# A decode step with a long KV cache: VectorE's loop border moved by half a block, two reorderings on VectorE and TensorE, and wider output rows

## The chip, the cores and the metric

The kernel runs on one core of a Trainium2 chip. The metric is device time in microseconds (us), the median of several executions of the whole program. A profile of one further execution shows when each instruction ran and when each transfer landed.

## The reference

One token (batch 1, sequence 1, width 1024) goes through an attention over a cache and a small mixer with an MLP, side by side, both from the same normalised input:

```python
def _A_ref(x, k_cache, v_cache, wq, wo):          # 32 query heads, 4 KV heads, 65536 keys, width 128
    q = (x @ wq).reshape(B, Sq, Hq, Dh) ...
    scores = jnp.einsum("bhqd,bhkd->bhqk", q, k) * (Dh ** -0.5)
    p = _softmax(scores, axis=-1)
    o = jnp.einsum("bhqk,bhkd->bhqd", p, v)
    return o... .reshape(B, Sq, Hq * Dh) @ wo

def _B_ref(x, w1, w2, w3, w4):
    h = _gelu(_layernorm(x, axis=-1) @ w1)
    ...                                            # shifts along the sequence, here of one token
    x1 = x + hs
    h2 = _gelu(_layernorm(x1, axis=-1) @ w3) @ w4  # 1024 -> 3584 -> 1024
    return x1 + h2

x = A_x
xn = _layernorm(x, axis=-1)
return x + _A_ref(xn, A_k_cache, A_v_cache, A_wq, A_wo) + _B_ref(xn, B_w1, B_w2, B_w3, B_w4)
```

Everything is bf16. The two caches are 67 MB each, and eight query heads share a KV head, so every byte of K and V is read once and used for eight short products.

## The kernel before

**Tiles and blocks.** The keys of a KV head are cut into 8 tiles of 8192, which makes `NT` = 32 tiles `n` for the 4 heads. Four tiles make a block. A block's V is one load of 8 MB into one of two V slots (`issue_v`, L335). Its K is two loads of 4 MB, one for tiles 0 and 1 of the block into K slot 0 and one for tiles 2 and 3 into K slot 1 (`issue_k`, L325). All loads go through SyncE's queue in program order, and each waits there until its slot is free: a K slot when the scores of its second tile have been computed, a V slot when the last products with it have.

**One tile**, in the order in which the loop (L580) writes it down:

- `Ttr(n, ...)` (L484) lets VectorE transpose the tile's K in place, in four pieces of 128x1024 (L489). K must be turned before TensorE can use it.
- `QK(n)` (L492) is 16 products on TensorE that write the scores to `S_ps`.
- `stats1`, `MB` and `stats2` find a bound for the exponents: VectorE takes the row maximum (L506) and spreads it (`Rm`, L507), TensorE combines the rows in a small product (L512), VectorE takes the minimum (L516).
- `EXP(n)` (L519) updates the running bound `brun` on VectorE, and ScalarE takes the exponentials into `p_sb` (L527).
- `PTr(n)` (L533) permutes them on TensorE (L535) and transposes them on VectorE (L537) into `pT_f`.
- `PV(n)` (L539) is 16 products with V on TensorE into `OT_ps`.
- `FLASH(n)` (L550) copies the result on ScalarE and adds it, rescaled, to `O_acc` on GpSimd. After 8 tiles `head_end` (L561) puts the head's result away, on GpSimd too.

**The order of the work** is written out by hand: each engine executes its own instructions strictly in the order of this loop, and waits on semaphores where it needs another engine or a load. VectorE works ahead: while tile `n` goes through its chain, the pieces of tile `ahead` = `n + 1` are transposed in between, the first one ahead of `stats1(n)`, the second behind `EXP(n)`, the last two behind `PTr(n)`. This is done within a block alone; the first tile of a block is transposed in one go at the block's start:

```python
if n % 4 == 0:
    q_dve.mark(const_sems)
    q_act.mark()
    Ttr(n, range(4))
ahead = n + 1 if n % 4 < 3 else None
```

**The loops.** `mark` (L49) notes where a loop's body begins. `emit_looped` (L68) turns the stretches between marks into a hardware loop, whose iterations must have the same instructions; what lies ahead of the first mark and behind the last is emitted straight. VectorE and ScalarE loop over blocks of four tiles, TensorE and GpSimd over heads of eight.

**The end.** Behind the last tile come the products with w1, w2 and w3 (`quad_rows`), the normalisation of the attention, and the output rows. `out_rows` (L448) multiplies one column (128 values of `gh_bf`, the MLP's hidden vector, or of `o_bf`, the attention's result) with a row of 1024 weights, as four products of 256 columns side by side in the four column groups of TensorE, each accumulating into its own partition of `OUT_ps`. `w4` has 28 such rows, in three loads of 16, 10 and 2 rows; `wo` has 32 in one load. The order on TensorE is 16 rows of `w4`, the 32 of `wo`, 10 and then 2 rows of `w4` (L671 to L674). The loads land in the same order. Then VectorE copies the sum (L675) and one transfer writes the output.

Of the kernel before, what the change touches and what calls it, by code (L numbers as in the profile page):

```python
# [7 lines left out]
F32 = mybir.dt.float32  # L8
ACTF = mybir.ActivationFunctionType
ALU = mybir.AluOpType  # L10
# [127 lines left out]
def _op(q, fn, reads=(), writes=(), partial=False, tick=True):  # L138
    _deps(q, reads, writes)
    ev = q.op(fn, tick)  # L140
    _done(ev, reads, writes, partial)
    return ev


def _grp(q, fns, reads=(), writes=(), partial=False):
    _deps(q, reads, writes)
    ev = None
    for i, fn in enumerate(fns):
        ev = q.op(fn, i == len(fns) - 1)
    _done(ev, reads, writes, partial)  # L150
    return ev
# [16 lines left out]
def bass_parallel_sum__gqa_block_cached__mixer_s_mlp__decode_kernel(  # L168
# [13 lines left out]
    P = 128  # L182
    D = A_x.shape[2]
# [9 lines left out]
    NT = HKV * NSUB  # L193
# [7 lines left out]
    with ExitStack() as es:  # L201
        E = es.enter_context

        def sb(name, shape, dt):
            return E(nc.sbuf_tensor(name, shape, dt))
# [8 lines left out]
        ones_f = sb("ones_f", [P, P], F32)  # L214
# [15 lines left out]
        xn3 = sb("xn3", [P, KT_D], F32)  # L230
        xn3_bf = sb("xn3_bf", [P, KT_D], BF)
        ln_s = sb("ln_s", [P, 8], F32)
        spare = sb("spare", [P, 4], F32)
        ln_xc = sb("ln_xc", [P, KT_D], F32)
        ln_sq = sb("ln_sq", [P, KT_D], F32)
        qT_bf = sb("qT_bf", [P, HQ], BF)
# [13 lines left out]
        ff = sb("ff", [P, 2], F32)  # L250
        cb_rL = sb("cb_rL", [P, HKV], F32)
        cb_o = sb("cb_o", [P, 32], F32)
        o_bf = sb("o_bf", [P, 32], BF)
        acc = sb("acc", [P, KT_D], F32)
        g_bf = sb("g_bf", [P, KT_D], BF)
        gh_bf = sb("gh_bf", [P, KT_F], BF)
        KV = sb("KV", [P, 98304], BF)
# [12 lines left out]
        OUT_ps = ps("OUT_ps", [P, 512], F32)  # L270
        S_ps = ps("S_ps", [P, 512], F32)
# [8 lines left out]
        q_pe = _Q("pe", sem("c_pe"), in_order=True)  # L280
        q_dve = _Q("dve", sem("c_dve"))
        q_act = _Q("act", sem("c_act"))
        q_pool = _Q("pool", sem("c_pool"))
# [11 lines left out]
        b_const = _B("const")  # L295
# [4 lines left out]
        b_V = [_B(), _B()]  # L300
        b_tmpO = _B(); b_tmpL = [_B(), _B()]; b_epi = _B(); b_CM = _B()
        b_S = _B(); b_PT = _B(); b_MB = _B(); b_OT = _B()
# [6 lines left out]
        b_OUT = _B()  # L309
        b_cb = _B()  # L310
        b_o = _B()
# [89 lines left out]
        for c0, n_, lhs, rhs in ((0, P, selGT[:, :], selGT[:, :]), (P, P, selGT[:, :], selPT[:, :]),  # L401
                                 (256, 4, selTT[:, :], ident_bf[0:4, 0:4]), (260, 16, selDT[:, :], ident_bf[0:16, 0:16])):
            _op(q_pe, lambda e, c0=c0, n_=n_, lhs=lhs, rhs=rhs: e.matmul(CM_ps[:, c0:c0 + n_], lhs, rhs, start=True, stop=True),
                reads=[b_const, b_pT], writes=[b_CM], partial=(c0 > 0))
# [7 lines left out]
        for j in range(KT_D):  # L412
            for b in range(2):
                for jj in range(4):
# [3 lines left out]
                        start=(j == 0), stop=(j == KT_D - 1), tile_position=(0, 32 * jj)))  # L418
# [9 lines left out]
        for h in range(HKV):  # L428
            for we in range(4):
# [3 lines left out]
                    reads=[b_M1, b_const], writes=[b_Y], partial=(h + we > 0))  # L433
# [3 lines left out]
        def head_switch(h):  # L437

            _deps(q_pool, [b_Y], [b_Yc])
            src = (lambda: Yall[:, HKV - 1, :, :, :]) if h == 0 else (lambda: Yall[:, bass.ds(q_pool.var, 1), :, :, :].rearrange("p o a b g -> p (o a) b g"))  # L440
            ev = q_pool.op(lambda e: e.tensor_copy(Ycur[:, :, :, :], src()), tick=(s_y, h + 1))
            _done(ev, [b_Y], [b_Yc])
            for b in (b_brun[1],):
                for s, v in list(b.w.items()) + list(b.r.items()):
                    q_pool.wait((s, v))
            q_pool.ops.append((2, lambda e: e.memset(brun[:, 1:2], BIG), s_b, 2))

        def out_rows(items, reads, last=False):  # L448
            fns = []
            for lhs, rhs in items:  # L450
                for jj in range(4):
                    fns.append(lambda e, lhs=lhs, rhs=rhs, jj=jj: e.matmul(  # L452
                        OUT_ps[32 * jj:32 * jj + 1, 0:256], lhs, rhs[:, 256 * jj:256 * jj + 256],
                        start=False, stop=last, tile_position=(0, 32 * jj), skip_group_check=True))
            _grp(q_pe, fns, reads=reads, writes=[b_OUT], partial=True)
# [26 lines left out]
        pT_bf = pT_f[:].bitcast(BF).rearrange("p (q r two) -> p q r two", q=16, two=2)  # L482

        def Ttr(n, idx):  # L484
            s, half = (n // 2) % 2, n % 2
            for ix in idx:
                c = KOFF[s] // 2 + 4096 * half + 1024 * ix
                _deps(q_dve, [b_K[s][half]], [])
                ev = q_dve.op(lambda e, c=c: e.transpose(out=KV32[:, c:c + 1024], in_=KV32[:, c:c + 1024]))  # L489
                b_T[s][half].add_write(ev)  # L490

        def QK(n):  # L492
            s, half = (n // 2) % 2, n % 2
            fns = []
            for we in range(4):
                w_hi, e_ = divmod(we, 2)
                for cm in range(4):
                    mv = bass.AP(KV[:].tensor, KOFF[s] + half * 8192 + cm * 128 + w_hi * 64 + e_, [[kstep, P], [512, 16], [2, 32]])
                    fns.append(lambda e, we=we, cm=cm, mv=mv: e.matmul(  # L499
                        S_ps[32 * cm:32 * cm + 32, :], Ycur[:, we, :, :].rearrange("p a g -> p (a g)"), mv,  # L500
                        start=(we == 0), stop=(we == 3), tile_position=(0, 32 * cm)))
            _grp(q_pe, fns, reads=[b_T[s][half], b_Yc], writes=[b_S])
# [36 lines left out]
        def PV(n):  # L539
            s, r = (n // VSUB) % 2, n % VSUB  # L540
            v0 = VOFF[s] + 8192 * r
            fns = []
            for q in range(16):
                q4 = q % 4
                fns.append(lambda e, q=q, q4=q4: e.matmul(OT_ps[32 * q4:32 * q4 + 32, :], pT_bf[:, q, :, 1],  # L545
                                                          KV[:, v0 + 512 * q:v0 + 512 * (q + 1)],
                                                          start=(q < 4), stop=(q >= 12), tile_position=(0, 32 * q4)))
            _grp(q_pe, fns, reads=[b_pT, b_V[s]], writes=[b_OT])

        def FLASH(n):  # L550

            m = n % 2
            _op(q_act, lambda e: e.activation(tmpO[:, 1:513], OT_ps[:, :], ACTF.Copy), reads=[b_OT], writes=[b_tmpO])  # L553
            _deps(q_pool, [b_ff[m]], [b_Oacc])
            q_pool.op(lambda e: e.tensor_tensor(out=spare[:, 0:1], in0=ff[:, m:m + 1], in1=ff[:, m:m + 1], op=ALU.add), False)  # L555
            b_Oacc.set_write(q_pool.op(lambda e: e.tensor_scalar(out=O_acc[:, :], in0=O_acc[:, :], scalar1=ff[:, m:m + 1], scalar2=0.0, op0=ALU.mult, op1=ALU.add)))  # L556
            _deps(q_pool, [b_tmpO, b_tmpL[m], b_Oacc], [])
            ev = q_pool.op(lambda e: e.tensor_tensor(out=O_acc[:, m:m + 513], in0=O_acc[:, m:m + 513], in1=tmpO[:, m:m + 513], op=ALU.add), tick=(s_fl, n + 5))  # L558
            _done(ev, [b_ff[m], b_tmpO, b_tmpL[m]], [b_Oacc])
# [20 lines left out]
        for n in range(NT):  # L580
            if n % NSUB == 0:
                q_pe.mark(const_sems)
                q_pool.mark()
            if n % 4 == 0:
                q_dve.mark(const_sems)
                q_act.mark()
                Ttr(n, range(4))
            ahead = n + 1 if n % 4 < 3 else None
            QK(n)
            if ahead:  # L590
                Ttr(ahead, [0])
            stats1(n)
            MB(n)
            stats2(n)
            EXP(n)
            if ahead:
                Ttr(ahead, [1])
            PTr(n)
            if ahead:
                Ttr(ahead, [2, 3])  # L600
            if n % NSUB == NSUB - 1:
                head_switch(n // NSUB + 1)
            PV(n)
            FLASH(n)
            if n % NSUB == NSUB - 1:
                head_end(n // NSUB)
            if n % 2:
                issue_k((n + 3) // 2)
            if n % 4 == 1:
                issue_v((n + 3) // 4)  # L610
            if n == NT - 3:
                load_at(KOFF[0], b_K[0][:1] + b_T[0], "w1", B_w1, 0, 8)
                load_at(KOFF[0] + 8192, b_K[0][1:], "w2", B_w2, 0, 8)
                b_epi.r.update(b_V[0].r)
                load_at(VOFF[0], [b_V[0]], "w3", B_w3, 0, 8)
            if n == NT - 1:
                load_at(KOFF[1], b_K[1] + b_T[1], "w40", B_w4, 0, 16)
                load_at(VOFF[1], [b_V[1]], "wo", A_wo, 0, 32)
        for q in (q_pe, q_pool, q_dve, q_act):
            q.mark(const_sems)  # L620

        quad_rows(M0_ps, [b_M0], (xn2_bf, b_xn2), KV[:, 0:8192], b_K[0][0], 256)
# [24 lines left out]
                        b_w.add_read((s, v))  # L647
                load_at(c0, [b_w], "w4%d" % i, B_w4, r0, nr)

        def w4_pe(i):  # L650
            r0, nr, c0, b_w = w4_parts[i]
            out_rows([(gh_bf[:, r:r + 1], KV[:, c0 + (r - r0) * D:c0 + (r - r0 + 1) * D]) for r in range(r0, r0 + nr)], [b_w, b_gh], last=(i == len(w4_parts) - 1))

        _op(q_dve, lambda e: e.tensor_copy(EPI[:, 1024:1280], CM_ps[:, 0:256]), reads=[b_CM], writes=b_ge)
        _op(q_pe, lambda e: e.matmul(MB_ps[:, 0:HKV], Dmat_f, keep[:, :, P], start=True, stop=True), reads=[b_keep] + b_ge, writes=[b_MB])
# [12 lines left out]
        _op(q_dve, lambda e: e.transpose(out=ghT, in_=MM_ps[:, :].rearrange("p (b c) -> p b c", b=2)[:, :, 0:448].rearrange("p b (i r) -> p r b i", r=28)),  # L668
            reads=[b_M0, b_M1], writes=b_ge)
        gelu(tmp_flat[:, 0:896:32], KT_F, gh_bf[:, :], b_ge, [b_gh], (ge_x, ge_a, ge_b), b_ge)  # L670
        w4_pe(0)  # L671
        out_rows([(o_bf[:, r:r + 1], wo_sb[:, r * D:(r + 1) * D]) for r in range(32)], [b_V[1], b_o])
        w4_pe(1)
        w4_pe(2)  # L674
        _op(q_dve, lambda e: e.tensor_copy(orow, OUT_ps[:, 0:256]), reads=[b_OUT], writes=[b_p[0]])  # L675
        ev_out = _dma(q_sp, chan("out"), lambda e: e.dma_start(out=out[0, 0, :].rearrange("(j n) -> j n", j=4), in_=orow[0:97:32, :]), reads=[b_p[0]])
        q_sp.wait(ev_out)
# [34 lines left out]
```

## Time and profile before

| | |
|---|---|
| time, median of 3 runs (range) | 409.73 us (408.55 to 411.58) |
| profiled execution: its own time | 412.34 us |
| profiled execution: span from first to last instruction | 410.8 us |
| busy: VectorE, TensorE, GpSimd, ScalarE | 230.7, 167.0, 91.8, 49.6 us |
| read from memory | 169.87 MB, 414 GB/s over the span |
| mean granted TensorE clock | 0.605 of full speed |
| one transpose of a K piece (L489), 128 of them | 1.21 us |
| K load, from issue to landing (median of 16) | 21.7 us |
| V load, from issue to landing (median of 8) | 33.5 us |

A row of the groups names line, engine and operation, then output and input with their shapes, and gives the mean duration of one. Idle time is followed by what ended it. Times in the timelines are us from the span's start. Loads and engines run beside each other, so the busy times don't add up to the span.

### The profile page before, as it was taken

The numbers are of one execution on the slowest core, as the hardware profiler recorded it, in microseconds if no ns is written. First come the engines' busy times: TensorE is split into PE (matmuls) and PEld (weight loads), VectorE is DVE, ScalarE is ACT, GpSimd is POOL, SyncE is SP. The second block draws the span as 40 slices with busy tenths as digits, with TensorE's granted clock in tenths as the row PEclk, the third lists the DMA queues.
The fourth block names the chain that finished last, engine by engine and source line by source line (L and its number), as shares of the span: only waits on it lengthen the run. The fifth ranks groups of instructions, "written<-read, shape, count | busy, mean of one in ns | idle before, by whom it ended". The sixth has DMA issues, their size and how long they took to land.

```text
span 410.8 us, 4789 instructions
## 1 busy us (share of the span) xinstructions
PE 167.0 (41%) x1544; PEld 53.7 (13%) x1560; DVE 230.7 (56%) x393; ACT 49.6 (12%) x132; POOL 91.8 (22%) x173
## 2 busy tenths in 40 slices
PE   0054234443443344334632453254415452554616
PEld 0022011110110011001110111011101110122303
DVE  0024747674867386848673868386648666644400
ACT  1000011111111011102111110112101111110000
POOL 6000021222234122212251222123412320342000
PEclk9997555655655665565655555565566555565868
DMA  9999999999998999999989999999999989999994
GB/s 402 415 405 412 458 409 456 415 433 380 440 474 373 396 463 415 421 377 459 447 380 392 459 421 405 351 456 421 444 373 428 485 373 370 461 420 450 442 397 174
DMA packets 4768, 169.99 MB, mean 414 GB/s; under 512 B 660, under 2 KB 664, under 8 KB 792
## 3 DMA queue, kind: packets, MB, share of 16 engines
q1 hardware_dynamic: 4616, 169.87, 97.3%
q8 instruction: 6, 0.10, 0.1%
q10 hardware_dynamic: 144, 0.00, 0.0%
q14 instruction: 2, 0.02, 0.0%
HBM read 169.87 MB, written 0.00 MB: 414 GB/s over the span
## 4 chain that ended last, share of the span: by engine, by line
DMA 53%; DVE 20%; PE 12%; issue 11%; another core or an unknown queue 2%; ACT 1%; DVEq 0%; POOL 0%; ACTq 0%; SPq 0%; POOLq 0%
DMA KV<-in_A_k_cache_dram 38%; DVE KV L489 13%; DMA KV<-in_B_w_dram 10%; PE S_ps L499 8%; DMA x_bf<-in_A_x_dram 5%; DVE mrow L506 3%; PE PT_ps L535 1%; DVE pT_f L537 1%; PE MB_ps L512 1%; DVE Rm L507 1%; DVE Bst L516 1%; DVE brun L525 1%; PE MM_ps L464 1%; ACT p_sb L527 1%
## 5 line engine op out<-in xcount | busy, mean ns | idle before, releaser
L489 DVE STREAM_TRANSPOSE KV<-KV 128x1024 f32<-128x1024 f32 x128 | 150.2, 1212 | 46.8 <-DMA KV<-in_A_k_cache_dram 46.8
L545 PE MATMUL OT_ps<-KV,pT_f 128*32 128x512 bf16 x512 | 60.7, 627 | 59.4 <-DVE pT_f L537 59.4
L499 PE MATMUL S_ps<-KV,Ycur 128*32 128x512 bf16 x512 | 59.7, 614 | 33.2 <-DVE KV L489 33.2
L558 POOL TENSOR_TENSOR O_acc<-O_acc,tmpO 128x513 f32<-128x513 f32 x32 | 40.9, 1279 | 100.9 <-ACT tmpO L553 100.9
L527 ACT ACTIVATE p_sb<-S_ps,brun 128x512 bf16<-128x512 f32 x32 | 22.0, 687 | 174.6 <-DVE brun L525 174.6
L506 DVE TENSOR_REDUCE mrow<-S_ps 128x1 f32<-128x512 f32 x32 | 21.8, 682 | 31.3 <-PE S_ps L499 31.3
L512 PE MATMUL MB_ps<-Rm,Lmat 128*128 128x16 bf16 x32 | 6.1, 192 | 74.0 <-DVE Rm L507 74.0
L555 POOL TENSOR_TENSOR spare<-ff 128x1 f32<-128x1 f32 x32 | 6.2, 195 | 133.4 <-ACT ff L531 133.1
L553 ACT ACTIVATE tmpO<-OT_ps 128x512 f32<-128x512 f32 x32 | 19.2, 600 | 110.5 <-PE OT_ps L545 110.5
L537 DVE STREAM_TRANSPOSE pT_f<-PT_ps 128x512 f32<-128x512 f32 x32 | 22.8, 712 | 12.2 <-PE PT_ps L535 9.4
L499 PEld LDWEIGHTS S_ps<-KV,Ycur 128*32 128x32 bf16 x512 | 14.5, 126 | 78.6 <-DVE KV L489 44.0
L556 POOL TENSOR_SCALAR O_acc<-O_acc,ff 128x514 f32<-128x514 f32 x32 | 22.5, 703 | 0.2 <-issue 0.2
L545 PEld LDWEIGHTS OT_ps<-KV,pT_f 128*32 128x32 bf16 x512 | 14.7, 128 | 58.2 <-DVE pT_f L537 35.7
L535 PE MATMUL PT_ps<-p_sb,permR 128*128 128x512 bf16 x16 | 9.3, 581 | 21.8 <-ACT p_sb L527 21.8
L512 PEld LDWEIGHTS MB_ps<-Rm,Lmat 128*128 128x128 bf16 x32 | 3.3, 102 | 101.9 <-DVE Rm L507 101.9
L381 PE MATMUL MM_ps<-ln_s,ones_f 128*128 128x1 f32 x6 | 1.8, 362 | 27.2 <-DVE ln_s L380 27.2
L377 DVE CAST xT<-x_bf 128x8 f32<-128x8 bf16 x1 | 0.2, 173 | 21.6 <-DMA x_bf<-in_A_x_dram 21.6
L675 DVE CAST p_sb<-OUT_ps 128x256 bf16<-128x256 f32 x1 | 0.4, 426 | 20.7 <-PE OUT_ps L452 20.7
L516 DVE TENSOR_REDUCE Bst<-MB_ps 128x1 f32<-128x16 f32 x32 | 5.6, 175 | 9.2 <-PE MB_ps L512 9.2
L393 POOL TENSOR_TENSOR ln_s<-ln_s,neghalf 128x1 f32<-128x1 f32 x3 | 1.7, 560 | 37.0 <-DVE ln_s L391 37.0
L452 PE MATMUL OUT_ps<-KV,o_bf 128*1 128x256 bf16 x128 | 6.0, 374 | 9.4 <-DMA KV<-in_A_wo_dram 9.4
L535 PEld LDWEIGHTS PT_ps<-p_sb,permR 128*128 128x128 bf16 x32 | 3.3, 103 | 49.0 <-ACT p_sb L527 49.0
(107 smaller groups left out, 118.7 us busy)
## 6 DMA issues: line engine op xcount, KB each, us to landing
KV<-in_A_k_cache_dram SPq DMA_DIRECT2D x16, 4096.0 KB, 21.7
KV<-in_B_w_dram SPq DMA_DIRECT2D x1, 7168.0 KB, 30.4
KV<-in_B_w_dram SPq DMA_DIRECT2D x2, 2048.0 KB, 11.7
KV<-in_B_w_dram SPq DMA_DIRECT2D x1, 4096.0 KB, 20.7
KV<-in_B_w_dram SPq DMA_DIRECT2D x1, 2560.0 KB, 39.2
KV<-in_B_w_dram SPq DMA_DIRECT2D x1, 512.0 KB, 40.1
KV<-in_A_v_cache_dram SPq DMA_DIRECT2D x8, 33.5
x_bf<-in_A_x_dram ACTq DMA_DIRECT2D x1, 2.0 KB, 22.2
```

What stands on the lines that cost most here:

```text
L489: ev = q_dve.op(lambda e, c=c: e.transpose(out=KV32[:, c:c + 1024], in_=KV32[:, c:c + 1024]))
L499: fns.append(lambda e, we=we, cm=cm, mv=mv: e.matmul(S_ps[32 * cm:32 * cm + 32, :], Ycur[:, we, :, :].rearrange("p a g -> p (a g)"), mv, s ...
L506: _op(q_dve, lambda e: e.reduce_max(mrow[:, m:m + 1], S_ps[:, :], axis=AX.X), reads=[b_S], writes=[b_mrow[m]])
L512: _op(q_pe, lambda e: e.matmul(MB_ps[:, 0:16], Lmat[:, :], Rm[:, m, :], start=True, stop=True), reads=[b_R[m], b_const], writes=[b_MB])
L516: _op(q_dve, lambda e: e.tensor_reduce(out=Bst[:, n % 4:n % 4 + 1], in_=MB_ps[:, 0:16], axis=AX.X, op=ALU.min), reads=[b_MB], writes=[b_Bc ...
L527: _op(q_act, lambda e: e.activation(p_sb[:, m, :], S_ps[:, :], ACTF.Exp, bias=brun[:, m:m + 1], scale=SCALE, accum_out=tmpO[:, cL:cL + 1]) ...
L535: _op(q_pe, lambda e: e.matmul(PT_ps[:, :], permR[:, :], p_sb[:, m, :], start=True, stop=True), reads=[b_p[m], b_const], writes=[b_PT])
L537: _op(q_dve, lambda e: e.transpose(out=pT_f[:, :], in_=PT_ps[:, :]), reads=[b_PT], writes=[b_pT])
L545: fns.append(lambda e, q=q, q4=q4: e.matmul(OT_ps[32 * q4:32 * q4 + 32, :], pT_bf[:, q, :, 1], KV[:, v0 + 512 * q:v0 + 512 * (q + 1)], sta ...
L553: _op(q_act, lambda e: e.activation(tmpO[:, 1:513], OT_ps[:, :], ACTF.Copy), reads=[b_OT], writes=[b_tmpO])
L556: b_Oacc.set_write(q_pool.op(lambda e: e.tensor_scalar(out=O_acc[:, :], in0=O_acc[:, :], scalar1=ff[:, m:m + 1], scalar2=0.0, op0=ALU.mult ...
L558: ev = q_pool.op(lambda e: e.tensor_tensor(out=O_acc[:, m:m + 513], in0=O_acc[:, m:m + 513], in1=tmpO[:, m:m + 513], op=ALU.add), tick=(s_ ...
```

## The change

- In the loop, VectorE's mark moves from the first tile of a block (`n % 4 == 0`) to its third (`n % 4 == 2`). ScalarE's mark stays.
- The pieces of the third tile are no longer transposed between the steps of the second, but in one go at the new mark. The first tile of the next block is transposed between the steps of the fourth.
- Behind the last tile there is no next one; there VectorE writes four single columns of `spare` with zeros. GpSimd's scratch column in `spare` moves from 0 to 4.
- In the first tile of a block, TensorE gets the scores of the second tile ahead of the V products of the first.
- The first 16 rows of `w4` and the 32 of `wo` are multiplied as two products of 512 columns in two column groups (`half_rows`), accumulating into two partitions of `S_ps`, which VectorE clears beforehand. VectorE copies these two rows, and four small products fold them into `OUT_ps` between the 10 and the 2 last rows of `w4`.

```diff
         def Ttr(n, idx):
+            if n >= NT:
+                for ix in idx:
+                    q_dve.op(lambda e, ix=ix: e.memset(spare[:, ix:ix + 1], 0.0))
+                return
...
             if n % 4 == 0:
+                q_act.mark()
+            if n % 4 == 2:
                 q_dve.mark(const_sems)
-                q_act.mark()
+            if n == 0 or n % 4 == 2:
                 Ttr(n, range(4))
-            ahead = n + 1 if n % 4 < 3 else None
-            QK(n)
+            ahead = n + 1 if n % 4 != 1 else None
+            if n % 4 != 1:
+                QK(n)
             if ahead:
                 Ttr(ahead, [0])
             stats1(n)
...
             if n % NSUB == NSUB - 1:
                 head_switch(n // NSUB + 1)
+            if n % 4 == 0:
+                QK(n + 1)
             PV(n)
...
-        for q in (q_pe, q_pool, q_dve, q_act):
+        for q in (q_pe, q_pool, q_act):
             q.mark(const_sems)
...
+        def half_rows(items, reads):
+
+            _grp(q_pe, [lambda e, lhs=lhs, rhs=rhs, jj=jj: e.matmul(
+                S_ps[32 * jj:32 * jj + 1, :], lhs, rhs[:, 512 * jj:512 * jj + 512],
+                start=False, stop=True, tile_position=(0, 32 * jj), skip_group_check=True)
+                for lhs, rhs in items for jj in range(2)], reads=reads, writes=[b_S], partial=True)
+
+        _op(q_dve, lambda e: e.memset(S_ps[0:64, :], 0.0), writes=[b_S])
...
-        w4_pe(0)
-        out_rows([(o_bf[:, r:r + 1], wo_sb[:, r * D:(r + 1) * D]) for r in range(32)], [b_V[1], b_o])
-        w4_pe(1)
-        w4_pe(2)
+        half_rows(*w4_rows(0))
+        half_rows([(o_bf[:, r:r + 1], wo_sb[:, r * D:(r + 1) * D]) for r in range(32)], [b_V[1], b_o])
+        halves = tmp_flat[0:64, 0:512]
+        _op(q_dve, lambda e: e.tensor_copy(halves, S_ps[0:64, :]), reads=[b_S], writes=b_ge)
+        out_rows(*w4_rows(1))
+        _grp(q_pe, [lambda e, jj=jj: e.matmul(OUT_ps[32 * jj:32 * jj + 1, 0:256], ones_f[32 * (jj // 2):32 * (jj // 2) + 1, 0:1],
+                                              tmp_flat[32 * (jj // 2):32 * (jj // 2) + 1, 256 * (jj % 2):256 * (jj % 2) + 256],
+                                              start=False, stop=False, tile_position=(32 * (jj // 2), 32 * jj), skip_group_check=True)
+                    for jj in range(4)], reads=b_ge + [b_const], writes=[b_OUT], partial=True)
+        out_rows(*w4_rows(2), last=True)
```

More of the change, by code (lines that the diff above doesn't have):

```diff
@@ L232, in bass_parallel_sum__gqa_block_cached__mixer_s_mlp__decode_kernel @@
         ln_s = sb("ln_s", [P, 8], F32)
-        spare = sb("spare", [P, 4], F32)
+        spare = sb("spare", [P, 5], F32)
         ln_xc = sb("ln_xc", [P, KT_D], F32)
@@ L554, in FLASH @@
             _deps(q_pool, [b_ff[m]], [b_Oacc])
-            q_pool.op(lambda e: e.tensor_tensor(out=spare[:, 0:1], in0=ff[:, m:m + 1], in1=ff[:, m:m + 1], op=ALU.add), False)
+            q_pool.op(lambda e: e.tensor_tensor(out=spare[:, 4:5], in0=ff[:, m:m + 1], in1=ff[:, m:m + 1], op=ALU.add), False)
             b_Oacc.set_write(q_pool.op(lambda e: e.tensor_scalar(out=O_acc[:, :], in0=O_acc[:, :], scalar1=ff[:, m:m + 1], scalar2=0.0, op0=ALU.mult, op1=ALU.add)))
@@ L648, in bass_parallel_sum__gqa_block_cached__mixer_s_mlp__decode_kernel, with w4_rows @@
                 load_at(c0, [b_w], "w4%d" % i, B_w4, r0, nr)
-        def w4_pe(i):
+        def w4_rows(i):
             r0, nr, c0, b_w = w4_parts[i]
-            out_rows([(gh_bf[:, r:r + 1], KV[:, c0 + (r - r0) * D:c0 + (r - r0 + 1) * D]) for r in range(r0, r0 + nr)], [b_w, b_gh], last=(i == len(w4_parts) - 1))
+            return [(gh_bf[:, r:r + 1], KV[:, c0 + (r - r0) * D:c0 + (r - r0 + 1) * D]) for r in range(r0, r0 + nr)], [b_w, b_gh]
+        def half_rows(items, reads):
[4 more added lines that the diff above has]
+        _op(q_dve, lambda e: e.memset(S_ps[0:64, :], 0.0), writes=[b_S])
         _op(q_dve, lambda e: e.tensor_copy(EPI[:, 1024:1280], CM_ps[:, 0:256]), reads=[b_CM], writes=b_ge)
```

## The prediction

> **What bounds the kernel now.** I read the page first: DMA is busy in every slice while VectorE is at 56% and TensorE at 41%. In a fence "..." marks lines left out.
>
> ```profile
> PE 167.0 (41%) x1544; PEld 53.7 (13%) x1560; DVE 230.7 (56%) x393; ACT 49.6 (12%) x132; POOL 91.8 (22%) x173
> ...
> HBM read 169.87 MB, written 0.00 MB: 414 GB/s over the span
> ```
>
> So time goes with bytes, and only moments when the transfers run below their best rate are to be had. A block of four tiles reads 16.78 MB (two K loads and one V load). Next, VectorE's timeline: each first transpose of a block's second half starts as its K lands. Call that landing L.
>
> ```profile
> 63.15 1.25 DVE L489 STREAM_TRANSPOSE KV<-KV 128x1024 f32<-128x1024 f32 x1 [7.35 <-DMA KV<-in_A_k_cache_dram]
> ...
> 101.92 1.25 DVE L489 STREAM_TRANSPOSE KV<-KV 128x1024 f32<-128x1024 f32 x1 [4.85 <-DMA KV<-in_A_k_cache_dram]
> 142.84 1.25 DVE L489 STREAM_TRANSPOSE KV<-KV 128x1024 f32<-128x1024 f32 x1 [6.66 <-DMA KV<-in_A_k_cache_dram]
> 182.15 1.25 DVE L489 STREAM_TRANSPOSE KV<-KV 128x1024 f32<-128x1024 f32 x1 [5.31 <-DMA KV<-in_A_k_cache_dram]
> ...
> 341.84 1.25 DVE L489 STREAM_TRANSPOSE KV<-KV 128x1024 f32<-128x1024 f32 x1 [4.95 <-DMA KV<-in_A_k_cache_dram]
> ```
>
> The first cycle takes 101.92 - 63.15 = 38.77 us, which is 433 GB/s. The next six average (341.84 - 101.92) / 6 = 39.99. Third, SyncE's timeline, for when the next block's loads are issued:
>
> ```profile
> 58.23 0.43 SPq L341 DMA_DIRECT2D KV<-in_A_v_cache_dram  x1
> ...
> 99.50 0.43 SPq L341 DMA_DIRECT2D KV<-in_A_v_cache_dram  x1
> ...
> 138.57 0.43 SPq L341 DMA_DIRECT2D KV<-in_A_v_cache_dram  x1
> ```
>
> The V issue (the K load is issued just ahead of it) leads L by 4.92, 2.42 and 4.27 us here, and by 2.88, 3.54, 3.31 and 3.66 at the later four. The cycles that follow these leads take 38.77, 40.92, 39.31, 40.40, 40.10, 40.08 and 39.11 us: a short lead makes a long cycle, nearly in order. Last, the table by stretches (time in us; the last two columns are DMA share and GB/s):
>
> ```profile
> 98.00:106.00 8.00, 1.65 (x14) 0.33 (x6) 3.50 (x7) 0.87 (x3) 1.26 (x3) 0.50 0.99 393
> ...
> 146.00:178.00 32.00, 16.01 (x129) 4.36 (x135) 23.71 (x34) 5.54 (x16) 7.80 (x12) 0.55 1.00 432
> 178.00:186.00 8.00, 1.19 (x10) 0.21 (x2) 3.28 (x7) 0.87 (x3) 0.80 (x2) 0.71 0.91 360
> ```
>
> Away from L the rate is 426 to 437; in the stretches around the seven later L it is 393, 385, 360, 385, 357, 352 and 344. The queue has too little behind the load that is ending.
>
> **The border on VectorE: the gain.** Now VectorE does a block in strict order: the first transpose for tile 2 stands ahead of tile 1's maximum, so tile 1's whole chain, and all behind it, waits for L. After L come tile 1's chain, tiles 2 and 3, and then tile 0 of the next block, whose transposes hide behind nothing (five in 5.71 us from 122.73). Its tile 1's scores end at 138.1, and they free the K slot: V issue at L + 36.65.
>
> After the change tile 1 is finished before L. From L: four transposes, three of them in a row taking 3.46 us, so 4.6; scores 1.93; tile 2's maximum starts at L + 6.55. From maximum to maximum a tile takes 7.9 us (the row of 103.09 to those of 111.00 and 118.93). That now holds for the next block's tile 0 as well, since its transposes lie inside tile 3. The scores of tiles 3, 0 and 1 end at L + 14.5, 22.4 and 30.3, and V is issued by L + 30.8. Lead: 38.77 - 30.8 = 8.0 us, above the 4.92 that went with the clean cycle. The K load behind tile 3 is issued 2.5 us sooner too; it already had a whole V load ahead of it.
>
> The gain: six cycles come back to 38.77, so 239.92 - 6 x 38.77 = 7.3 us, and the seventh border (L = 341.84, where the weight loads follow) about as much as a mean one, 1.2. Sum **8.5 us**. A second way: (431 - rate) / 431 x length over the seven border stretches (8 us each, the fifth 10) gives 0.71, 0.85, 1.32, 0.85, 1.72, 1.47, 1.61, together 8.5. Bounds 7.5 to 9.5; below, all that a lead of 8 us might still leave is nothing saved at all, kept as a rival.
>
> A row against a rule: at a lead of 4.27 us the next cycle was still 0.54 longer than the clean one. The Trainium skill ("DMA: Bandwidth & Descriptors", section Latency and other measured facts) gives some 0.6 us to the first byte of a transfer issued from SyncE. By that alone every lead seen here sufficed, the borders had another cause and this term would be nothing; the order of leads and cycles speaks for the trace.
>
> **Costs of that part.** VectorE's jump back now falls where it waits for L. Extra waits: tile 2 is transposed wholly after L (three more transposes, 3.5 us), and that is in the chain above. VectorE's slack must hold it: tile 1's scores end at L + 30.3, its maximum and Rm take 0.9, and then TensorE's small product (MB) is queued behind the 16 V products that were moved behind the scores. These run to about L + 32.3, so MB waits about 1 us; MB to the end of the tile's pT took 2.9 us (119.89 to 122.81), so VectorE is through at L + 35.2 and has 3.6 us in hand. If that cover goes, each us more is 7 us in all. The order itself: now the first V products run at 134.06, and scores wait for transposes to 136.2 anyway, so nothing is gained there today. Afterwards it matters. V lands 33.0 us or more after its issue, about L + 30 now and L + 29 to 30 afterwards. Left in front, the products would be due at L + 26 and hold the scores for some 3.5 us. Next block's K is on chip at about L + 10.5 and first touched at L + 12.6. The four tiny memsets of VectorE behind the last tile, the moved scratch column on GpSimd and the clearing of S_ps cost at most 1 us, in the 11 us between the GELU (388.0) and wo (399.3); the last tiles end some 2.5 us sooner after their L as well.
>
> **The tail: a loss.** Here the tail's PE rows, and the clock (the column before the last two):
>
> ```profile
> 399.34 5.99 PE L452 MATMUL OUT_ps<-KV,o_bf 128*1 128x256 bf16 x128 [9.37 <-DMA KV<-in_A_wo_dram]
> 406.95 1.64 PE L452 MATMUL OUT_ps<-KV,gh_bf 128*1 128x256 bf16 x48 [1.61 <-DMA KV<-in_B_w_dram]
> ...
> 390.00:404.20 14.20, 4.86 (x96) 3.12 (x100) 0.00 (x0) 0.00 (x0) 0.00 (x0) 0.64 0.92 393
> 404.20:410.80 6.60, 2.77 (x89) 1.65 (x80) 0.43 (x1) 0.00 (x0) 0.00 (x0) 1.00 0.14 54
> ```
>
> The wo rows end at 405.33, 1.6 us ahead of the next weights. A row is now four products of 256 columns side by side: 92 products in 4.76 us at clock 0.50, 0.207 us a row, and 0.109 a row at 1.00. Afterwards it is two of 512 on two of the four column groups: half as many instructions, each streaming twice as long, so about 0.414 and 0.218 a row. No row here has two groups only; below, 0.109 and 0.207 if the columns were free, above these doubles. I take the doubles, since the 64 narrow products at full clock took 1.92 us, four side by side, which is streaming and not issue.
>
> The clock went to 1.00 at 404.2, 4.8 us into wo, after 9.4 us idle. If so again: 4.8 / 0.414 = 11.6 rows at half and 20.4 x 0.218 = 4.4 us, wo 9.2 us, ending at 408.6 on the old time axis. Ten w4 rows, 1.2; the four folding products, half of the 1.03 that L636 took at half clock, 0.55 (the copy of the halves, 0.69 by L660, lies beside the ten rows); the last two rows 0.35: TensorE ends at 410.7 in place of 408.6, **+2.1 us**. All at full clock, wo ends at 406.3 and the fold alone is left: +0.3. All at half: 13.2 us for wo, 2.1, 1.0 and 0.6 behind it: +7.7. The first 16 w4 rows take 3.5 to 7 us inside the idle time.
>
> The Trainium skill ("TensorE: Matmul & The Clock Gate", section What's actually happening) says that the full clock comes after one busy window of 3.4 us and goes after an idle one. By that wo runs 3.4 to 6.8 us at half, and this term would be +1.5 to +3.1 as an estimate.
>
> **Sum.** 412.34 (the profiled execution, 1.5 over its span) - 8.5 + 2.1 = 405.9. It stands 2.6 over the median; from the median 409.73 the same sum gives **403.3**.
>
> **Rivals.** *Half clock to the end (12%).* Two column groups might not count as busy enough; against it, wo at clock 0.50 got the full clock within 4.8 us. 409.73 - 8.5 + 7.7 = 408.9. *The borders stay (10%):* the loss is a matter of the change from one K slot to the other and not of the lead; for it, the dip sits just behind L each time; against it, the first L. 409.73 + 2.1 = 411.8. *VectorE becomes the bound, slower (5%).* Its chain needs 35.2 of 38.77 us. For it: the period now lengthens to 10.7 us where GpSimd's end of a head runs beside the tile (118.93 to 129.67). One such period among the three makes 38.0, still hidden; two make 40.8, seven cycles 2.0 longer each: 403.3 + 14 = 417. It decides from a chain of 38.8 on and ends slower from 40.3. Against it: most of those 10.7 is transposing that is now covered.
>
> **Numbers.** The forecast has 73%; its own range is 401 to 405.9. To hold 8 in 10 I go up to the half-clock case: 400.8 to 409. A measurement of this kernel tells about 1% from no change, 405.6 to 413.8. Faster 0.70 (nearly all of the forecast's chance), same 0.23 (its upper edge, half clock, borders that stay), slower 0.07.
>
> **What would show it.** Right: V issues about 8 us ahead of L, seven cycles of 38.6 to 39, about 430 GB/s around L, VectorE idle some 3 us ahead of each L, wo in 64 products of about 9 us, followed at once by the ten rows. Wrong: cycles near 40 with leads of 8 us (borders); VectorE without idle time ahead of L (bound); the clock at 0.50 until the end (tail).

## The result, and the profile after

| | before | after |
|---|---|---|
| time, median (range) | 410.02 us (408.55 to 411.58, 4 runs) | 405.70 us (405.56 to 405.86, 4 runs) |
| profiled execution: time, span | 412.34, 410.8 | 405.76, 404.5 |
| mean cycle between landings L | 39.81 | 38.78 |
| wo lands | 399.30 | 390.38 |
| last w4 rows land | 408.15 | 397.72 |
| TensorE's last product ends | 408.6 | 402.3 |

The ratio is 0.9894, with a 95% interval of 0.9857 to 0.9932: the time fell by about 1%. That is clear of the spread, but less than the 2% from which a change counts as faster here; it counts as the same. The forecast was 403.3, with a range of 400.8 to 409.0. The executions after lie within 0.3 us of each other; those before are spread over 3 us here, and from 405.38 to 411.65 in 18 of the 19 that ran beside the experiments (one, 411.96, is counted as slow and left out).

The page of after: TensorE is busy 5.8 us longer with 72 recorded products fewer, the other engines do much the same work, and the rate over the span is up from 414 to 420 GB/s.

```profile
PE 172.8 (43%) x1472; PEld 53.3 (13%) x1472; DVE 233.4 (58%) x399; ACT 48.6 (12%) x132; POOL 91.3 (23%) x173
...
HBM read 169.87 MB, written 0.00 MB: 420 GB/s over the span
```

VectorE's timeline after, at the landings L:

```profile
63.13 5.75 DVE L493 STREAM_TRANSPOSE KV<-KV 128x1024 f32<-128x1024 f32 x5 [2.27 <-DMA KV<-in_A_k_cache_dram]
...
101.91 5.75 DVE L493 STREAM_TRANSPOSE KV<-KV 128x1024 f32<-128x1024 f32 x5 [3.46 <-DMA KV<-in_A_k_cache_dram]
140.69 5.75 DVE L493 STREAM_TRANSPOSE KV<-KV 128x1024 f32<-128x1024 f32 x5 [3.00 <-DMA KV<-in_A_k_cache_dram]
```

Every cycle is now 38.77 to 38.80 us, as the first one was before. VectorE transposes five pieces in a row (four of tile 2, one of tile 3), and had been idle for 3.0 to 3.5 us at each L from the second on. SyncE's timeline after, for the same two L:

```profile
94.55 0.43 SPq L341 DMA_DIRECT2D KV<-in_A_v_cache_dram  x1
...
133.57 0.43 SPq L341 DMA_DIRECT2D KV<-in_A_v_cache_dram  x1
```

The V load leads L by 7.36 and 7.12 us (2.42 and 4.27 before). The table by stretches after, with DMA share and GB/s last:

```profile
146.00:178.00 32.00, 16.43 (x132) 4.21 (x124) 21.22 (x36) 5.49 (x16) 7.29 (x11) 0.55 0.99 429
178.00:186.00 8.00, 1.86 (x16) 0.45 (x16) 5.75 (x5) 0.28 (x1) 1.27 (x1) 0.50 1.04 446
```

The stretch around L, 360 GB/s before, is no slower than the rest. So the loop part did what it was to do. The end did not:

```profile
390.43 9.53 PE L665 MATMUL S_ps<-KV,o_bf 128*1 128x512 bf16 x60 [9.41 <-DMA KV<-in_A_wo_dram]
...
401.41 0.61 PE L694 MATMUL OUT_ps<-KV,ones_f 1*1 1x256 f32 x8
401.94 0.39 PE L452 MATMUL OUT_ps<-KV,gh_bf 128*1 128x256 bf16 x8
```

The last weights are on chip at 397.72, and TensorE goes on until 402.3: 4.6 us behind the last landing, where it was 0.4 before.

### The profile page after: what moved, and what is told of

Its sections match the earlier page's. It is cut to its first block, busy times and chain, and to the rows that moved or that the text cites. A ratio compares the mean times of both kernels' runs of the same rounds, so it can differ in the third digit from the quotient of the medians.

```text
span 404.5 us, 4599 instructions
## 1 busy us (share of the span) xinstructions
PE 172.8 (43%) x1472; PEld 53.3 (13%) x1472; DVE 233.4 (58%) x399; ACT 48.6 (12%) x132; POOL 91.3 (23%) x173
## 4 chain that ended last, share of the span: by engine, by line
DMA 56%; DVE 18%; PE 15%; issue 9%; ACT 1%; another core or an unknown queue 1%; DVEq 0%; POOL 0%; ACTq 0%; SPq 0%; POOLq 0%
DMA KV<-in_A_k_cache_dram 41%; DVE KV L493 13%; DMA KV<-in_A_wo_dram 9%; PE S_ps L503 8%; DMA x_bf<-in_A_x_dram 5%; PE S_ps L665 2%; DVE mrow L510 2%; PE PT_ps L539 2%; PE OT_ps L549 1%; ACT p_sb L531 1%; DVE pT_f L541 1%; PE MB_ps L516 1%; DVE Rm L511 0%; DVE Bst L520 0%
## 5 line engine op out<-in xcount | busy, mean ns | idle before, releaser
L549 PE MATMUL OT_ps<-KV,pT_f 128*32 128x512 bf16 x512 | 56.6, 590 | 19.5 <-DVE pT_f L541 18.6
L539 PE MATMUL PT_ps<-p_sb,permR 128*128 128x512 bf16 x32 | 17.0, 533 | 45.2 <-ACT p_sb L531 45.2
L665 PE MATMUL S_ps<-KV,o_bf 128*1 128x512 bf16 x64 | 10.0, 486 | 9.4 <-DMA KV<-in_A_wo_dram 9.4
L393 POOL TENSOR_TENSOR ln_s<-ln_s,neghalf 128x1 f32<-128x1 f32 x3 | 1.7, 558 | 36.4 <-DVE ln_s L391 36.4
## 6 DMA issues: line engine op xcount, KB each, us to landing
KV<-in_B_w_dram SPq DMA_DIRECT2D x1, 7168.0 KB, 33.2
```

What stands on the lines that cost most here:

```text
L539: _op(q_pe, lambda e: e.matmul(PT_ps[:, :], permR[:, :], p_sb[:, m, :], start=True, stop=True), reads=[b_p[m], b_const], writes=[b_PT])
L665: _grp(q_pe, [lambda e, lhs=lhs, rhs=rhs, jj=jj: e.matmul(S_ps[32 * jj:32 * jj + 1, :], lhs, rhs[:, 512 * jj:512 * jj + 512], start=False, ...
```

## Experiments

Two theories. **Lead:** the loss at the borders comes from loads that are issued too shortly ahead of the end of the one in flight, and all that matters of the loop part is when the next block's loads are issued. **Tail:** the wide rows cost time. The rivals are stated with each run.

### The loop part without the wide rows

```diff
-        half_rows(*w4_rows(0))
-        half_rows([... wo ...])
-        ...                                  # copy and fold of the halves
+        out_rows(*w4_rows(0))
+        out_rows([... wo ...], [b_V[1], b_o])
         out_rows(*w4_rows(1))
```

> Both changes to the loop, with the end as it was (all output rows as four products of 256 columns). Theory: the loop alone gives the whole gain, and the wide rows lose part of it: TensorE ends some 0.5 us behind the last landing, as before, in place of 4.6. wo from 390.4 takes 6.0 us again and ends just as the next weights land (396.5), so the span is about 400.4 and the time 401.6, some 4 below the changed kernel and 8.5 below the one before. Rival (the wide rows cost nothing, or the rest of the gain was lost in the loop): 405.7, as the changed kernel.

Measured: 401.71 us (401.64 to 403.02), ratio to before 0.9813 (0.9783 to 0.9843), span 400.4. It is faster than both kernels and the fastest of this study, 4.0 us below the changed kernel. TensorE's timeline at its end:

```profile
390.47 5.34 PE L452 MATMUL OUT_ps<-KV,o_bf 128*1 128x256 bf16 x128 [10.78 <-DMA KV<-in_A_wo_dram]
396.57 1.64 PE L452 MATMUL OUT_ps<-KV,gh_bf 128*1 128x256 bf16 x48 [0.76 <-DMA KV<-in_B_w_dram]
```

wo lands where it does after the change, and its rows are through before the next weights land at 396.52. The whole gain is the loop's, and the wide rows give 4.0 us of it back.

### The wide rows without the loop part

The kernel before, with `half_rows`, the copy and the fold.

> The loop as before, with the wide output rows. Theory: wo takes 9 to 10 us in place of 6.0, so TensorE ends 2 to 3 us later relative to wo's landing: 410.0 + 2.5 = 412.5. Cycles between landings stay at 39 to 41 us. Rival (half as many instructions save something): 409 or less.

Measured: 412.94 us (411.09 to 414.39), ratio 1.0053 (1.0029 to 1.0078). TensorE ends 11.7 us behind wo's landing (410.73 against 399.01), 9.3 in the profile of before: +2.4, as the theory had it. TensorE's timeline at its end:

```profile
399.05 9.30 PE L656 MATMUL S_ps<-KV,o_bf 128*1 128x512 bf16 x60 [6.71 <-DMA KV<-in_A_wo_dram]
...
410.35 0.39 PE L452 MATMUL OUT_ps<-KV,gh_bf 128*1 128x256 bf16 x8
```

### Is it the clock that makes the wide rows slow?

```diff
+        _grp(q_pe, [lambda e: e.matmul(PT_ps[:, :], permR[:, :], KV[:, VOFF[0]:VOFF[0] + 512],
+                                       start=True, stop=True) for _ in range(40)],
+             reads=[b_V[0], b_const], writes=[b_PT])
         half_rows([... wo ...])
```

> The changed kernel with 40 products of 128 x 512 into an unused bank ahead of the wo rows, to keep TensorE busy in the 9 us that it idles there. They are extra work; the output does not depend on them. Theory: the clock is at full speed when wo lands, so its 64 wide products take 7.0 us in place of 9.8 and the time falls by about 2.8 us, to 403. Rival (the wide rows are bound by something other than the clock): 405.7 or more.

Measured: 403.38 us (402.91 to 404.80), ratio 0.9848 (0.9774 to 0.9923), 2.3 below the changed kernel. First the stretches of the changed kernel (the clock is the third column from the end), then TensorE's rows with the extra products, and the stretch of wo there:

```profile
390.40:396.30 5.90, 5.87 (x28) 1.81 (x30) 0.00 (x0) 0.00 (x0) 0.00 (x0) 0.50 0.87 366
396.30:400.20 3.90, 3.90 (x44) 1.57 (x42) 0.00 (x0) 0.00 (x0) 0.00 (x0) 1.00 0.05 21
```

```profile
382.45 8.81 PE L690 MATMUL PT_ps<-KV,permR 128*128 128x512 bf16 x40
391.19 6.64 PE L665 MATMUL S_ps<-KV,o_bf 128*1 128x512 bf16 x60
```

```profile
391.20:397.90 6.70, 6.70 (x71) 2.72 (x72) 0.00 (x0) 0.00 (x0) 0.00 (x0) 1.00 0.69 289
```

With the clock at 1.00, 60 of the 64 wo products take 6.64 us in place of 9.53. The extra products ran 0.7 us past the landing of wo, which is most of what is missing from the 2.8 expected. Even at full clock the 64 wide products need about 7.1 us (6.64 x 64 / 60), 1.0 more than the 6.1 that the next weights need behind wo, and copy and fold come after them.

### TensorE's order taken back

```diff
-            if n % 4 != 1:
-                QK(n)
+            QK(n)
...
-            if n % 4 == 0:
-                QK(n + 1)
             PV(n)
```

> The changed kernel, with the V products of a block's first tile ahead of the second tile's scores again. Theory: these products are due some 26 us after L but wait for V until about 29; the scores then end at about 33 and the lead of the loads falls from 7 to about 5.5 us, which is still enough: within 1 us of 405.7, cycles 38.8 to 39.0. Rival (the order of TensorE is what the gain rests on): leads below 4 us, cycles near 40, 411 or more.

Measured: 405.66 us (404.28 to 406.42), ratio 0.9905 (0.9878 to 0.9932). V issues 32.9 to 33.3 us after L (31.4 to 31.8 in the changed kernel), leads are 5.5 to 5.9, cycles 38.77 to 38.83. The order moves the issue by about 1.5 us, where the prediction had 3.5, and the median by less than the executions scatter.

### TensorE's order alone

The kernel before, with the lines that the experiment above takes out put in.

> The kernel before, with TensorE's new order alone (scores of a block's second tile ahead of the first tile's V products). Theory: those scores wait for transposes that end later than the products would, so they end at the same time, 36 us after L; leads 2.4 to 4.3 us and cycles of about 40 us as before, 410 within the spread of the kernel before. Rival (the order frees the K slot sooner by the 1.9 us of the products): leads some 2 us longer, cycles near 39.

Measured: one run, 406.47 us. V issues 36.2 to 37.1 us after L, as before (36.4 to 36.9), so the order by itself frees the K slot no sooner: the theory held there. But the time is at the fast edge of the kernel before, and four of the seven cycles take 38.75 to 38.83 us, three of them after leads of only 1.9 to 4.1 us, so the expectation of cycles near 40 did not hold:

```profile
220.43 1.25 DVE L489 STREAM_TRANSPOSE KV<-KV 128x1024 f32<-128x1024 f32 x1 [4.35 <-DMA KV<-in_A_k_cache_dram]
259.26 1.25 DVE L489 STREAM_TRANSPOSE KV<-KV 128x1024 f32<-128x1024 f32 x1 [4.69 <-DMA KV<-in_A_k_cache_dram]
298.05 1.25 DVE L489 STREAM_TRANSPOSE KV<-KV 128x1024 f32<-128x1024 f32 x1 [4.15 <-DMA KV<-in_A_k_cache_dram]
```

The lead at 259.26 is 2.26 us, and the next cycle takes 38.79. The lead as I had measured it is therefore not the whole of it; see below.

### One part of VectorE's order

```diff
             if n % 4 == 0:
                 q_dve.mark(const_sems)
                 q_act.mark()
+            if n % 2 == 0:
                 Ttr(n, range(4))
-            ahead = n + 1 if n % 4 < 3 else None
+            ahead = n + 1 if n % 2 == 0 else None
```

> The kernel before, with one half of VectorE's new order: the third tile is transposed in one go after the second tile is done, and no tile is transposed ahead across either border, so the first tile of a block is still transposed in the open. Loop mark, TensorE's order and the end as before. Theory: from L, scores of the third tile end at 6.6, of the fourth at 14.5, of the next first tile at 14.5 + 10.7 = 25.2 and of its second at 33.2, so the lead is about 5 us and most of the border loss is gone: 402 to 404. Rival (transposing the next block's first tile ahead is needed): lead below 4 us, cycles near 40, 409 to 411.

Measured: 402.09 us (401.86 to 403.90), ratio 0.9826 (0.9791 to 0.9860). One line of the kernel before is added and one is altered, and with the end as it was they do as well as the whole loop part. V issues 33.6 to 34.4 us after L (33.2 expected), leads are 4.3 to 5.2, and all cycles take 38.76 to 38.81. VectorE's timeline shows what the rest of the change is good for:

```profile
101.79 5.75 DVE L489 STREAM_TRANSPOSE KV<-KV 128x1024 f32<-128x1024 f32 x5 [1.76 <-DMA KV<-in_A_k_cache_dram]
140.60 5.75 DVE L489 STREAM_TRANSPOSE KV<-KV 128x1024 f32<-128x1024 f32 x5 [1.54 <-DMA KV<-in_A_k_cache_dram]
```

Idle time ahead of L is 1.1 to 1.8 us here and 3.0 to 3.5 in the changed kernel. Transposing across the border buys reserve, not time.

### The loads issued late on purpose

```diff
-            PV(n)
+            ev_pv = PV(n)
             FLASH(n)
+            if n % 4 == 1:
+                q_sp.wait(ev_pv)
```

> The changed kernel with one more wait: SyncE issues the next block's first K load and its V load only after the V products of the block's second tile, some 6 us later than it could. Nothing else is changed, so this tests the lead by itself. Theory: the lead falls to about 3 us, cycles rise from 38.78 to about 40.3, and the time by seven times 1.5 us to about 416. Rival (the border loss has to do with VectorE's order or with the change of slots): cycles stay at 38.8, 405.7.

Measured: one run, 414.61 us, mean cycle 39.97. The first border shows it best: VectorE's timeline has a cycle of 42.11 us behind it, and SyncE's has the V load issued behind L.

```profile
62.72 5.75 DVE L493 STREAM_TRANSPOSE KV<-KV 128x1024 f32<-128x1024 f32 x5 [1.29 <-DMA KV<-in_A_k_cache_dram]
104.83 5.75 DVE L493 STREAM_TRANSPOSE KV<-KV 128x1024 f32<-128x1024 f32 x5 [4.90 <-DMA KV<-in_A_k_cache_dram]
```

```profile
62.95 0.43 SPq L341 DMA_DIRECT2D KV<-in_A_v_cache_dram  x1
```

VectorE's order is that of the changed kernel, yet the loss at the borders is back: it belongs to the lead. Here too two of the cycles are nearly clean (38.96 and 38.79, after leads of 2.96 and 2.60).

### The kernel before once more

> The kernel before, profiled once more. The profiled execution of before took 412.34 us and lies above its median of 410.0; the changed kernel's executions lie within 0.3 us of each other. Theory: the loss at the borders varies from one execution to the next, and an execution near the median has shorter cycles, a mean of 39.6 rather than 40.0. Rival: the profile itself costs it 2 us, and the mean cycle stays at 40.0 whatever the time.

Measured: one run, 411.10 us, mean cycle 39.68. The cycles go with the time: 7 x (39.81 - 39.68) = 0.9 us of the 1.2 between the two profiled executions of before. The changed kernel's profiled execution (405.76) lies among its others, so profiling costs it nothing that shows. An execution of before exactly at its median was not caught.

### What sets the loss at a border

A K load is carried by 16 DMA engines, and the trace records when each of them reports its share as done. L is the last of the 16. The table sets the V issue against the first one too; the next K load, which stands ahead of V in the queue, is issued 0.37 us earlier each time. The loss is 20 us less the bytes that the transfers' packets carried in the 20 us around L (from 6 before to 14 after) over 434 GB/s.

```
kernel               L      lead to the last   spread of the 16   lead to the first   loss, us
late issue          62.7        -0.26               1.61               -1.86            3.33
late issue         183.8         0.64               1.76               -1.12            2.34
before             262.6         3.28               3.03                0.25            1.94
before             142.8         4.25               3.00                1.24            1.08
order alone        259.2         2.24               0.55                1.69            0.06
late issue         224.0         2.60               0.56                2.04            0.04
half border        218.1         4.34               1.84                2.49            0.09
before              63.1         4.89               2.11                2.79            0.21
after              179.4         6.96               2.06                4.90            0.09
```

By the lead to the last engine, 2.24 us can be free and 4.25 cost 1.08. By the lead to the first, the free borders and the costly ones fall apart: of the first seven borders in each of the ten profiles, 70 in all, the 40 with 2 us or more lose at most 0.5 (all but the first border of a run at most 0.15), the 28 with less than 1.5 us lose 0.5 or more, and the two between lose 0.06 and 0.14. A cycle, which runs from last engine to last engine, hides a loss where the spread shrinks: the one behind 220.43 in TensorE's order alone takes 38.83 us, but its border lost 1.1 while the spread fell from 1.8 to 0.55. Within the 28 the loss does not follow the lead closely (1.13 us at a lead of 0.11, 1.67 at 1.25). The last border of each profile, behind which weights are loaded, is not counted: there a lead of 1.67 lost 1.0 in the wide rows without the loop part, and one of 2.63 or more lost 0.2 at most. The reading is that an engine that is through with its share and finds nothing behind it stands still, and that the spread decides how early that is; the packets in the trace don't name their engine, so no engine was seen standing still. The spread was 1.6 to 3.6 us in most places. It was about 0.55 at the two borders where a lead below 3 us to the last engine came out clean, and 0.5 to 0.75 at three that lost 0.5 to 1.1. What makes the spread shrink or grow was not tried.

The Trainium skill ("DMA: Bandwidth & Descriptors", section Latency and other measured facts) has about 0.6 us to the first byte on this kind of queue. Leads to the first engine of 0.7 to 1.5 us (0.37 more for the K load) still lost 0.5 to 1.9 us here, so for how early the next load must be issued the measurement decides.

## Why the prediction was right or wrong

**Right: the mechanism, and every cycle.** The loss sat where the next loads are issued too late (counted, as it turned out, from the first DMA engine to finish and not from the landing), and finishing tile 1 ahead of L removed it: 38.78 us for each cycle against 38.77 predicted, and at wo's landing a gain of 8.9 us (399.30 - 390.38) against 8.5. The late issue (the changed kernel's order with the loss back) and the half border (another order without the loss) are what show that it is the issue and not VectorE's order as such.

**Right, with a size off: the lead.** The tile's period was taken as 7.9 us from the profile of before. It is 8.1 after (maxima at 147.50, 155.64, 163.77 and 172.05), so V issues 31.4 to 31.8 us after L and not 30.8, and the lead is 7.0 to 7.4 from the second L on, not 8.0. There was room for that. The products moved behind the scores held up MB by 0.7 us (about 1 predicted):

```profile
170.10 1.90 PE L503 MATMUL S_ps<-KV,Ycur 128*32 128x512 bf16 x16 [3.06 <-DVE KV L493]
171.79 1.92 PE L549 MATMUL OT_ps<-KV,pT_f 128*32 128x512 bf16 x16
...
173.64 0.19 PE L516 MATMUL MB_ps<-Rm,Lmat 128*128 128x16 bf16 x1
```

VectorE's reserve came out at 3.0 to 3.5 us, 3.6 predicted, and V lands 29.1 us after L as worked out. The rival in which VectorE becomes the bound had nothing to show for itself; how much more work VectorE would bear was not tried.

**The tail: right in sign, and the term that was mis-sized.** The price of a wide row came out as the sum had it: 28 products took 5.87 us at clock 0.50, 0.42 us a row (0.414 predicted), and 60 took 6.64 us at 1.00 with the extra products ahead of them, 0.22 a row (0.218). Between wo's landing and TensorE's end there are now 12.0 us and were 9.3: +2.7 in place of +2.1. The difference is the clock: it stayed at 0.50 for 5.9 us of wo and not for 4.8, and each of these 1.1 us does half the work. (The Trainium skill, "TensorE: Matmul & The Clock Gate", section What's actually happening, allows the 5.9, by one busy window of 3.4 us that need not start with the work.) What the sum did not see is larger. It took the distance from wo's landing to the end of a narrow tail as fixed. That distance was 9.3 us before, because the last weights came 8.9 behind wo (408.15 - 399.30). In the loop part without the wide rows they came 7.4 behind it (397.78 - 390.43), and TensorE ended 7.8 behind it. Against that end the wide rows cost 4.0 us (405.70 - 401.71), and the sum had 2.1. Why the last weights came sooner stays open. The spread of the engines at the ten rows' landing went from 3.7 to 2.1 us, but the loop part need not be the reason: TensorE's order alone had 7.4 us too, without it.

**The sum: near the profiled execution, and by luck.** From the profiled execution the sum gave 405.9, and the profiled execution after took 405.76. Two errors cancel there: at the last landing the loop part had gained 10.4 us (408.15 - 397.72) and not 8.5, and the wide rows cost 4.0 and not 2.1. From the median the sum gave 403.3, and the median was 405.70: 4.3 us were gained where 6.4 were forecast. At the medians the loop part alone gained 8.3 us (410.02 - 401.71), close to the 8.5, so what is missing there is the tail's term, 4.0 in place of 2.1. That the 8.5 fits the median is luck as well. It was worked out from one execution 2.3 us above the median, and "from the median 409.73 the same sum gives 403.3" takes the loss at the borders for the same in every execution, while the kernel before varied over 6 us.

**The rivals.** Half clock to the end did not happen: the full clock came after 5.9 us. The borders did not stay. The range held the time, but at the upper edge of the forecast's own 401 to 405.9. And 405.70 lies just inside the 405.6 to 413.8 that the prediction could not tell from no change: it is the outcome "same", which had 0.23, and not "faster", which had 0.70.

## What to carry to other kernels

In a kernel that is bound by its transfers, look at when each load is issued against the end of the one in flight, and count from the first DMA engine to run dry: two microseconds of lead to it were enough here (at most 0.5 us lost), while to the landing 4.87 us was once too little. What an engine that works strictly in order can finish ahead of a late landing decides whether that lead is there. When a change takes away a loss that varies between executions, forecast the floor that remains, from bytes and the fixed ends, and don't subtract one execution's loss from another's median. Count what a row costs and not its instructions: half as many products, each of twice the width and in two column groups in place of four, took 0.42 us a row where the narrow ones took 0.207 at the same clock, and cost 4 us at the end, where nothing was left to hide it.

## What was not expected of the hardware

Loads in a single queue lost up to 2 us at a border although the next load was issued 2.2 to 4.9 us ahead of the landing; the 16 engines finished 1.6 to 3.6 us apart there, and what told the costly borders from the free ones was the lead to the first of them. The kernel before ran between 405.4 and 411.7 us. Its two profiled executions and that of TensorE's order alone (412.34, 411.10 and 406.47 us) differ mostly in how the loads land: between the first and the third, 2.1 us lie in the seven cycles, 1.7 between the last L, a border too, and wo's landing, and 1.5, with the cause open, between wo and the last weights. No execution of the kernel before near 405 us was profiled. Long leads don't make the time fixed either: the changed kernel ran within 0.3 us, but other kernels with clean cycles varied by 1.4 us (the loop part without the wide rows) to 2.1 us (TensorE's order taken back).
